# Causal attention ahead of two FFNs: units of 64 queries with both heads stacked on the partitions

## The chip, the cores and the metric

The kernel runs on one core of a Trainium2 chip. The metric is device time in microseconds (us) of one execution, lower is better; the time of before is the median of three runs. The engines are named as the profile names them: PE (TensorE matmuls), PEld (its weight loads), DVE (VectorE), ACT (ScalarE), POOL (GpSimd), SP (SyncE, whose queue issues the DMAs).

## The reference

Batch 2, 12 heads, 448 tokens, 64 elements per head, everything float32 from end to end. Attention is followed by two feed-forward networks.

```python
scores = q @ k.T / sqrt(64)                       # per head
scores = where(key > query, -1e9, scores)         # causal mask
attn = exp(scores - max(scores))
attn = attn / (sum(attn) + 1e-9)
x = (attn @ v)                                    # to [896 tokens, 768]
h = x @ w_in;  x = (h * sigmoid(h)) @ w_out       # 768 -> 2048 -> 768
h = x @ w_in2; solu = h * softmax(h)
x = layernorm(solu) * g @ w_out2                  # 768 -> 1024 -> 768
```

## The kernel before, in words

The kernel has three stages one after another: attention (to about 76 us), the first FFN, the second FFN. The FFNs multiply float32 numbers as sums of three products of rounded parts (`wh`, `wl` for a weight, `h`, `l` for an activation), and their weights arrive packed and have to be converted on ACT, DVE and POOL. The change touches the attention stage and how much of the weight conversion is done in it.

Attention runs over 12 **pairs** of heads (2 batches, 6 pairs each; `p` in the code). A pair's q and k lie with head 0 on partitions 0 to 63 and head 1 on 64 to 127. The work of a pair is cut into seven **units**. In the kernel before these are, for each of the two heads, a unit of 128 queries by 128, by 256 and by 384 keys, and one last unit with the remaining 64 queries of both heads by 448 keys, stacked on the partitions. The steps for a pair, each named by letters in a table:

- `So`, `Sa`, `Sb`, `Sc`: scores on PE (`scores`, L174; the last unit `scores_last`, L184). A matmul uses the 64 rows of its head, which is half of PE's array. The last unit is done in two passes that add into the same tile, and between the passes stands a relay through SP (`f`, L193), so that the two row halves don't write one bank at a time.
- `m`: mask and maximum of a unit, DVE (`maxes`, L204). It reads the scores from PSUM and writes scaled scores to `e` in SBUF.
- `e`: exponential with its row sum, ACT (`exps`, L210).
- `r`: one reciprocal of all the row sums of a pair, DVE (`recip`, L216 and L217).
- `n`: division of a unit by its sum, on POOL (L224), ACT (L222) or DVE (L226), as the letter G, A or V at the step's end says.
- `T`: 16 transposes on PE into one PSUM slot (`transp`, L238), twice per pair. `x`: their eviction to `aT`, on DVE (L253) or ACT (L255).
- `P`: the products with v on PE (`pv`, L264). `h` and `l`: their rounded part (ACT L273, DVE L271) and the rest (DVE L278), which are the input of the first FFN.

Beside these the table holds the loads (`q` L148, `v` L154, `w` L285, all issued by SP in order), steps of the weight conversion for the first FFN (`ca` on ACT, L291; `sh`, `sl`, `rh` on DVE, L308, L296 and L303; `sp` on ACT, L354; `wl` on POOL, L358) and, near the end of the stage, the first blocks of the FFN's first product (`g`, L427 to L429). A chunk of weights is 384 columns on 128 partitions.

The order of all these steps is the string `ORDER` (L60). The engines work off the instructions in the order in which the steps stand there, each engine its own share, and semaphores hold a step back until what it reads is there and what it overwrites is free. Scores, transposes and products with v share four PSUM slots of two banks each (the number after the slash); there are four buffers `e`, four `aT`, four for raw weights.

```python
        for step in ORDER.split():
            step, _, n = step.partition("/")
            e = {"A": nc.scalar, "V": nc.vector, "G": nc.gpsimd}.get(step[-1])
            ...
            emit[name](int(step[len(name):]), int(n) if n else None, u, e)
        fed[0] = EARLY + 1
        pend.append(EARLY)
```

Of the kernel before, what the change touches and what calls it, by code (L numbers as in the profile page):

```python
# [51 lines left out]
UNITS = [(0, 2), (1, 2), (0, 0), (1, 0), (0, 1), (1, 1), (0, 3)]  # L52

# [7 lines left out]
So0/1 Sa0/2 m0.00 m0.10 e0.00 Sb0/0 m0.02 m0.12 e0.02 f0 v5 Sc0 e0.12 v3 e0.10 m0.03 q4 v6 m0.01 Sa1/3 e0.03 m0.11  # L61
e0.01 Sb1/1 m1.10 e0.11 Sb2/2 m1.00 f1 m1.12 v0 Sc1 e1.00 f2 r0 w0 e1.10 m1.02 Sa2/0 n0.10G e1.12 m1.03 n0.12G e1.02
Sc2 m1.11 n0.03G m1.01 e1.03 m2.10 Sa3/3 m2.00 e1.11 m2.12 n0.00G n0.11G e1.01 m2.03 Sb3/1 e2.00 n0.02G m2.02 f3 Sc3
e2.10 m2.11 e2.03 n0.01G r1 Sb4/0 m3.02 e2.11 n1.11G f4 m2.01 q5 e2.12 n1.03G m3.10 v1 T0.0/2 m3.12 e2.02 v7 m3.00
n1.02G m3.11 w1 e2.01 T0.1/3 m3.03 v2 x0.0A Sc4 n1.12G m3.01 v9 r2 x0.1A n1.01G Sa4/1 x0.2V ca0 e3.03 n2.01G x0.3V
T1.1/2 q8 n1.00G e3.10 m4.00 w2 P0/3 m4.10 n2.03G e3.01 m4.01 w3 m4.11 e3.00 m4.03 n2.00G q6 e3.02 n1.10G m4.02
e3.12 n2.11G T1.0/0 m4.12 h0A n2.02G x1.3V Sa5/1 e3.11 n2.12G l0 x1.1A x1.0A x1.2V T2.1/3 n2.10G e4.02 r3 T2.0/0
m5.00 n3.10G e4.11 sh0 P1/2 n3.00G x2.1A x2.3V x2.0A n3.11G m5.12 n3.02G e4.12 x2.2V P2/0 e4.03 m5.10 n3.12G m5.02
h1A sl0 n3.01G e4.10 l1 e4.00 Sb5/3 e4.01 h2V n3.03G T3.0/1 e5.12 f5 q7 r4 T3.1/2 sh1 n4.12G ca3 l2 Sc5 e5.00 x3.2V
x3.0A n4.02G Sa6/0 x3.3V q9 x3.1A n4.11G e5.10 m5.11 Sb6/1 ca1 m6.00 n4.01G m6.12 P3/2 f6 e5.02 v4 n4.03G m5.03  # L70
e5.11 m5.01 e5.03 n4.10G m6.10 m6.02 n4.00G e5.01 T4.1/3 rh0 h3A T4.0/0 sh2 r5 x4.3A Sc6 l3 n5.01G x4.2A sl1 x4.0A
n5.00G Sa7/2 q10 m6.01 x4.1A m6.03 n5.10G e6.12 P4/3 n5.11G m7.00 m6.11 e6.00 n5.12G m7.12 e6.02 m7.02 n5.02G e6.01
m7.10 Sb7/0 h4V e6.10 n5.03G T5.0/1 e7.02 f7 v10 l4 Sc7 e6.11 x5.0V e7.12 T5.1/2 x5.1V e6.03 Sb8/3 rh1 Sa8/1 x5.3A
f8 w4 r6 m7.01 x5.2A n6.02G Sc8 m7.03 e7.00 e7.10 m7.11 n6.01G P5/2 m8.01 e7.01 n6.12G m8.10 sp1 m8.03 e7.11 n6.11G
m8.12 e7.03 m8.02 n6.10G Sa9/0 n6.00G m8.11 h5A n6.03G m8.00 sp0 l5 T6.0/3 e8.01 r7 Sb9/1 e8.12 x6.1V T6.1/2 n7.11G
f9 x6.0V v11 e8.10 Sc9 n7.01G w5 x6.3A m9.02 n7.02G v8 x6.2A P6/3 m9.10 q11 e8.11 m9.11 n7.03G m9.01 n7.00A e8.00
m9.00 n7.12V n7.10G e8.02 m9.03 T7.1/2 wl1 e8.03 m9.12 T7.0/1 x7.2A r8 Sa10/0 x7.3A x7.0V n8.00G n8.10G h6A Sb10/2
n8.01G e9.12 x7.1V m10.00 f10 n8.12G P7/1 l6 e9.10 e9.03 m10.12 n8.11G m10.10 e9.02 n8.02V n8.03G m10.02 e9.00
# [11 lines left out]
def fused(ctx, tc, qk, vv, w1, w2, w3, w4, gl, out):  # L90
# [13 lines left out]
    gain = const.tile([128, KF2], F32, name="gain")  # L104

# [16 lines left out]
    with tc.manual_schedule():  # L122
# [4 lines left out]
        mask3 = att.tile([128, S], F32, name="mask3", bufs=1)  # L127
# [48 lines left out]
        def scores_last(p, n, first):  # L176
            k, q = raws[p]
            if first:
                sb[p] = slot(n)
            dst = scs[p, 0, 3] = sb[p][:, :, 256:256 + S // 2]  # L180
            made = []
            for j in range(2):
                r, z = slice(64 * j, 64 * j + 64), j if first else 1 - j
                made.append(nc.tensor.matmul(dst[:, z], q[QC][r], k[r, S // 2 * z:S // 2 * (z + 1)],  # L184
                                             start=first, stop=not first))
            if first:
                passes[p] = made
            else:
                for m in made:
                    behind(m, relays[p])  # L190

        def relay(p):
            relays[p] = nc.sync.nop(nofuse=True)  # L193
            for m in passes[p]:
                behind(relays[p], m)
# [981 lines left out]
```

## Time and profile before

| | |
|---|---|
| median of 3 runs | 401.11 us (400.26 to 401.73) |
| the profiled execution | 401.01 us |
| its span in the profile | 399.2 us, TensorE clock 1.00 |
| PE, DVE, ACT, POOL busy | 98%, 74%, 70%, 46% of the span |
| DMA | 50.04 MB, mean 125 GB/s |

The profile is one execution. An engine counts as busy from the start of an instruction to its end, and for PE that can hold waits, since matmuls are pipelined. Shares over the whole span average three stages with different limits, so the rows below are taken from windows of the attention stage, and from one window of the FFN for comparison.

### The profile page before, as it was taken

What the parts mean: (1) busy time and instruction counts of PE and PEld (TensorE: products, weight loads), DVE (VectorE), ACT (ScalarE), POOL (GpSimd) and SP (SyncE); (2) the same over time, 40 slices, a digit from 0 to 9 for tenths busy, and PEclk for the clock granted to TensorE, in tenths of its full rate; (3) what the DMA queues carried; (4) which work ended last, traced back from release to release, by engine and by line L of the source; (5) the groups of instructions that cost most, each with busy time, mean ns of one, the idle gap of its engine ahead of it and who ended that gap; (6) DMA issues with size and microseconds to landing.
All of it is one profiled execution on the core that took longest, in us unless ns stands there. A gap on an engine that the chain in (4) does not pass through costs nothing.

```text
span 399.2 us, 7580 instructions
## 1 busy us (share of the span) xinstructions
PE 392.2 (98%) x2622; PEld 363.1 (91%) x2622; DVE 295.9 (74%) x693; ACT 281.1 (70%) x653; POOL 183.9 (46%) x219
## 2 busy tenths in 40 slices
PE   7999999999999999999999999999999999999996
PEld 5777678899999999999999999999988888999996
DVE  4999999677675765768566667776899997666943
ACT  5999999655665473766577777785757875898630
POOL 2998783223554372556665445554001000496450
PEclk9999999999999999999999999999999999999999
DMA  7775322134434333437344567777023320011121
GB/s 246 248 276 173 121 91 65 56 92 151 150 98 125 112 113 112 120 120 201 115 150 129 164 178 233 244 252 217 18 81 98 101 79 0 2 61 39 42 79 61
DMA packets 19766, 50.04 MB, mean 125 GB/s; under 512 B 2320, under 2 KB 4496, under 8 KB 19728
## 3 DMA queue, kind: packets, MB, share of 16 engines
q1 hardware_dynamic: 19728, 49.56, 39.4%
q8 instruction: 21, 0.34, 0.4%
q14 instruction: 17, 0.14, 0.1%
HBM read 46.80 MB, written 2.75 MB: 124 GB/s over the span
## 4 chain that ended last, share of the span: by engine, by line
PE 89%; DVE 8%; ACT 2%; issue 1%; DVEq 0%; ACTq 0%; SPq 0%
PE h L427 8%; PE h L429 8%; PE h L428 8%; PE x L264 5%; PE ps L942 5%; PE h L598 4%; PE h L597 4%; PE h L599 4%; PE ps L944 4%; PE ps L943 4%; PE h L865 3%; PE h L867 3%; PE h L866 3%; PE x L174 3%; PE x L238 3%; DVE e L204 3%
## 5 line engine op out<-in xcount | busy, mean ns | idle before, releaser
L291 ACT ACTIVATE wr<-wr 128x384 f32<-128x384 f32 x96 | 56.9, 592 | 9.4 <-DMA wr<-w_in 9.4
L428 PE MATMUL h<-l,wh 128*128 128x448 f32 x174 | 61.3, 352 | 0.0
L427 PE MATMUL h<-h,wh 128*128 128x448 f32 x174 | 61.3, 352 | 0.0
L429 PE MATMUL h<-h,wl 128*128 128x448 f32 x174 | 61.3, 352 | 0.0
L224 POOL TENSOR_TENSOR e<-e,st 128x128 f32<-128x128 f32 (+3 forms) x70 | 44.0, 666 | 20.1 <-DVE st L217 15.1
L321 DVE SCALAR_TENSOR_TENSOR pw<-wr,pw 128x384 uint32<-128x384 uint32 x77 | 43.0, 559 | 12.9 <-ACT pw L317 12.7
L446 POOL TENSOR_TENSOR gl<-sg,gh 128x448 fp32r<-128x448 f32 x29 | 32.8, 1152 | 38.9 <-ACT sg L444 38.9
L210 ACT ACTIVATE e<-e,st 128x128 f32<-128x128 f32 (+3 forms) x84 | 43.8, 536 | 4.2 <-DVE st L204 4.2
L358 DVE TENSOR_TENSOR wl<-pw,wh 128x384 fp32r<-128x384 f32 x29 | 16.2, 557 | 31.7 <-ACT wh L354 31.7
L354 ACT ACTIVATE wh<-pw 128x384 fp32r<-128x384 f32 x29 | 14.3, 494 | 35.2 <-PE h L428 27.4
L204 DVE CUSTOM_DVE_ANT_0 e<-x,mask 128x128 f32<-128x128 f32 (+3 forms) x84 | 32.9, 445 | 5.2 <-PE x L174 5.1
L428 PEld LDWEIGHTS h<-l,wh 128*128 128x128 f32 x174 | 32.9, 189 | 0.1
L427 PEld LDWEIGHTS h<-h,wh 128*128 128x128 f32 x174 | 32.9, 189 | 0.0
L429 PEld LDWEIGHTS h<-h,wl 128*128 128x128 f32 x174 | 32.9, 189 | 0.0
L896 POOL TENSOR_TENSOR s<-s,mhalf 128x1 f32<-128x1 f32 x7 | 4.2, 596 | 62.3 <-DVE s L895 62.3
L865 PE MATMUL h<-w3h,h 128*128 128x512 f32 x84 | 32.0, 381 | 0.6 <-ACT h L893 0.6
L866 PE MATMUL h<-w3l,h 128*128 128x512 f32 x84 | 31.9, 379 | 0.0
L867 PE MATMUL h<-w3h,l 128*128 128x512 f32 x84 | 31.8, 379 | 0.0
L597 PE MATMUL h<-gh,wh 128*128 128x448 f32 x90 | 31.7, 352 | 0.0
L599 PE MATMUL h<-gh,wl 128*128 128x448 f32 x90 | 31.7, 352 | 0.0
L598 PE MATMUL h<-gl,wh 128*128 128x448 f32 x90 | 31.7, 352 | 0.0
L358 POOL TENSOR_TENSOR wl<-wx,wh 128x384 fp32r<-128x384 f32 x21 | 21.2, 1011 | 22.7 <-ACT wh L354 22.7
(299 smaller groups left out, 1115.1 us busy)
## 6 DMA issues: line engine op xcount, KB each, us to landing
wr<-w_in SPq DMA_DIRECT2D x96, 384.0 KB, 3.2
qk<-qk_in SPq DMA_DIRECT2D x11, 480.0 KB, 4.6
v<-vv_in SPq DMA_DIRECT2D x12, 256.0 KB, 5.2
out<-o SPq DMA_DIRECT2D x14, 192.0 KB, 1.9
qk<-qk_in SPq DMA_DIRECT2D x2, 128.0 KB, 2.3
qk<-qk_in SPq DMA_DIRECT2D x1, 224.0 KB, 2.6
gain<-gl_in SPq DMA_DIRECT2D x1, 4.0 KB, 3.8
```

The lines of the kernel that those rows point to most:

```text
L204: nc.vector.tensor_tensor_reduce(o, scs[p, u[0], u[1]], m, -SCALE, 3.0e38, ALU.add, ALU.min, st[p % 4][:, COL[u]:COL[u] + 1])
L210: nc.scalar.activation(ep(p, u), ep(p, u), AF.Exp, bias=st[p % 4][:, n:n + 1], scale=-1.0, accum_out=st[p % 4][:, 8 + n:9 + n])
L224: eng.tensor_tensor(ep(p, u), ep(p, u), r.to_broadcast([128, wide(u[1])]), ALU.mult)
L291: nc.scalar.activation(high, high, AF.Copy, scale=DOWN)
L427: nc.tensor.matmul(ps[:, :S], wh, rh, start=turn == 0 and k % NB == 0, stop=False)
L428: nc.tensor.matmul(ps[:, :S], wh, rl, start=False, stop=False)
L429: nc.tensor.matmul(ps[:, :S], wl, rh, start=False, stop=turn == 1 and k % NB == NB - 1)
L597: nc.tensor.matmul(ps[:, :S], wh, rh, start=f == CF[0], stop=False)
L598: nc.tensor.matmul(ps[:, :S], wh, rl, start=False, stop=False)
L599: nc.tensor.matmul(ps[:, :S], wl, rh, start=False, stop=f == CF[-1])
L865: nc.tensor.matmul(ps[:, n], yh[k][:, at], wh, start=k == 0, stop=False)
L866: nc.tensor.matmul(ps[:, n], yh[k][:, at], wl, start=False, stop=False)
```

## The change

A unit now holds 64 queries of both heads, head 0 on partitions 0 to 63 of the result and head 1 on 64 to 127. A pair has seven units of 64, 128, ... 448 keys. The scores of a unit are two matmuls of 64 rows by 64 columns of the array; in units 1 to 4 (`SWAPPED`) the heads change places, so that head 0 writes partitions 64 to 127. Unswapped units go to the first bank of each slot, swapped ones to the second (`BANKS`). With that the two passes of the last unit, the relay and the second mask are gone, and q and k of a pair are 448 KB instead of 480.

```diff
-UNITS = [(0, 2), (1, 2), (0, 0), (1, 0), (0, 1), (1, 1), (0, 3)]
+UNITS = S // C
+SWAPPED = (1, 2, 3, 4)
+BANKS = ((6, 0), (4, 2), (5,), (3, 1))
+RUNS = ((0, 1, 0), (1, 5, 1), (5, 7, 0))
...
-        def scores(p, c):
-            k, q = raws[p]
-            for j in range(2):
-                r = slice(64 * j, 64 * j + 64)
-                t = sb[p][:, 1 - j] if c == 1 else sa[p][:, j, 384:] if c == 0 else sa[p][:, j]
-                scs[p, j, c] = dst = t[:, :wide(c)]
-                nc.tensor.matmul(dst, q[c][r], k[r, :wide(c)], start=True, stop=True)
...
+        def scores(p, us):
+            a = raws[p]
+            for u in us:
+                n = next(n for n, bank in enumerate(BANKS) if u in bank)
+                t = (sa, sb)[n // 2][p][:, n % 2]
+                o = sum(wide(v) for v in BANKS[n][:BANKS[n].index(u)])
+                scs[p, u] = t = t[:, o:o + wide(u)]
+                for j in range(2):
+                    r, z = slice(64 * j, 64 * j + 64), 64 * (j ^ (u in SWAPPED))
+                    nc.tensor.matmul(t[z:z + 64], a[r, 0, C * u:C * u + C], a[r, 1, :wide(u)], start=True, stop=True)
```

The products with v follow the swap: three runs of units with one assignment of heads each, 16 matmuls per pair instead of 8, over the same columns. Transposes are evicted by block of keys: pieces of 896, 128, 640 and 384 columns instead of 768, 256, 512 and 512.

```diff
             for z in range(NKB):
-                for j in range(2):
-                    nc.tensor.matmul(t[64 * j:64 * j + 64, 128 * z:S], v[:, j, z], aT[p][:, z, j, 128 * z:],
-                                     start=z == 0, stop=z == NKB - 1)
+                for lo, hi, swap in RUNS:
+                    sl = slice(C * max(lo, 2 * z), C * hi)
+                    for h in range(2):
+                        j = h ^ swap
+                        if sl.start < sl.stop:
+                            nc.tensor.matmul(t[64 * j:64 * j + 64, sl], v[:, j, z], aT[p][:, z, h, sl],
+                                             start=z == lo == 0, stop=z == NKB - 1, skip_group_check=True)
```

The first step of the weight conversion, `ca`, may be put on POOL, as a multiplication by a constant tile `down`; and four chunks instead of five are converted ahead of the FFN stage.

```diff
-        def conv_a(n, c):
+        def conv_a(n, c, eng=None):
             r = wraw[n, c]
             high = r[:, :, 1].bitcast(F32)
-            nc.scalar.activation(high, high, AF.Copy, scale=DOWN)
+            if eng is nc.gpsimd:
+                eng.tensor_tensor(high, high, down.to_broadcast([128, CH]), ALU.mult)
+            else:
+                nc.scalar.activation(high, high, AF.Copy, scale=DOWN)
...
-        fed[0] = EARLY + 1
-        pend.append(EARLY)
+        fed[0] = EARLY
```

The table is written anew throughout: another order, another share of the engines (norms, up to the last reciprocal: 64 columns on ACT, 1152 on DVE, the rest on POOL; `ca0` to `ca4` on POOL; `h9` to `h11` on DVE), loads in the order q1 v0 q2 v1 q3. One line of it:

```diff
-e2.10 m2.11 e2.03 n0.01G r1 Sb4/0 m3.02 e2.11 n1.11G f4 m2.01 q5 e2.12 n1.03G m3.10 v1 T0.0/2 m3.12 e2.02 v7 m3.00
+Sb4/3 x1.2V x1.1A n2.5G e3.6 P1/0 m4.2 q8 m4.1 n2.3G e3.5 m4.5 v7 m4.4 ca0G e4.1 r3 e4.4 m4.3 T2.1/2 n3.1G n3.4V h1A
```

On PE, one pair early in the stage; `x` is a PSUM slot, `qk` a pair's q and k, `e` its exponentials, `aT` the transposes, `v` its v. Before:

```order
L184 MATMUL x_258<-qk 128x224 x2
L174 MATMUL x_258<-qk 128x256 x2
L174 MATMUL x_334<-qk 128x384 x2
L174 MATMUL x_334<-qk 128x128 x2
L238 MATMUL x_344<-ident,e_98 128x64 x16
L264 MATMUL x_368<-aT,v_196 64x448 x2
L264 MATMUL x_368<-aT,v_196 64x320 x2
L264 MATMUL x_368<-aT,v_196 64x192 x2
L264 MATMUL x_368<-aT,v_196 64x64 x2
```

and now:

```order
L160 MATMUL x_311<-qk 64x448 x2
L160 MATMUL x_311<-qk 64x320 x2
L160 MATMUL x_311<-qk 64x192 x2
L160 MATMUL x_311<-qk 64x64 x2
L160 MATMUL x_324<-qk 64x384 x2
L160 MATMUL x_324<-qk 64x256 x2
L160 MATMUL x_324<-qk 64x128 x2
L225 MATMUL x_336<-aT,v_146 64x64 x2
L225 MATMUL x_336<-aT,v_146 64x256 x2
L225 MATMUL x_336<-aT,v_146 64x128 x2
L225 MATMUL x_336<-aT,v_146 64x192 x2
```

The result of a scores matmul now has 64 partitions instead of 128 (its first number), seven pairs of matmuls stand together where the passes of L184 were apart, and the products with v come in more and shorter pieces.

The step `ca` early in the table stood on ACT among the exponentials (`wr` is a chunk of raw weights):

```order
L210 ACTIVATE e_97,st_101<-e_97,st_101 128x256
L210 ACTIVATE e_98,st_102<-e_98,st_102 128x384
L291 ACTIVATE wr<-wr 128x384
L210 ACTIVATE e_98,st_102<-e_98,st_102 128x128
L255 ACTIVATE aT<-x_514 128x2x384
L255 ACTIVATE aT<-x_514 128x2x128
```

and stands now on POOL, between the norms of one pair and the next:

```order
L184 TENSOR_TENSOR e_99<-e_99,st_103 128x384
L184 TENSOR_TENSOR e_99<-e_99,st_103 128x256
L253 TENSOR_TENSOR wr<-wr,down 128x384
L184 TENSOR_TENSOR e_100<-e_100,st_104 128x128
L184 TENSOR_TENSOR e_100<-e_100,st_104 128x192
```

Norms that stood behind `ca` in no queue now stand behind it on POOL.

## Rows read from the trace of the kernel before

**Rows 1.** Windows: length, busy PE, PEld, DVE, ACT, POOL, clock, DMA share, GB/s.

```profile
4.50:16.65 12.15, 10.80 (x96) 7.72 (x92) 10.08 (x55) 10.41 (x39) 5.81 (x10) 1.00 0.76 274
16.65:62.15 45.50, 45.32 (x605) 33.25 (x605) 44.80 (x169) 45.37 (x151) 36.91 (x58) 1.00 0.49 167
...
80.00:100.00 20.00, 20.00 (x107) 19.98 (x106) 14.93 (x30) 11.43 (x27) 5.75 (x6) 1.00 0.41 123
```

**Rows 2.** The chain in order of time, one pair: start us, us, what.

```profile
28.78 0.99 PE x L238 x32
29.77 0.43 PE x L184 x4
30.21 1.30 PE x L174 x12
31.51 0.38 PE x L184 x4
31.89 1.88 PE x L264 x16
```

**Rows 3.** Groups by shape on ACT, 3 to 77 us: busy us, mean ns, idle before.

```profile
L210 ACT ACTIVATE e<-e,st 128x384 f32<-128x384 f32 x24 | 14.8, 620 | 0.9 <-DVE st L204 0.9
...
L210 ACT ACTIVATE e<-e,st 128x128 f32<-128x128 f32 x24 | 9.6, 406 | 2.8 <-DVE st L204 2.8
...
L273 ACT ACTIVATE h<-x 128x448 fp32r<-128x448 f32 x8 | 4.3, 542 | 3.8 <-PE x L264 3.8
```

**Rows 4.** Groups by shape on DVE, 3 to 77 us.

```profile
L204 DVE CUSTOM_DVE_ANT_0 e<-x,mask 128x384 f32<-128x384 f32 x24 | 12.8, 547 | 0.6 <-PE x L174 0.6
...
L253 DVE COPY aT<-x 128x512 f32<-128x512 f32 x14 | 9.2, 676 | 0.6 <-PE x L238 0.6
...
L278 DVE TENSOR_TENSOR l<-x,h 128x448 fp32r<-128x448 f32 x12 | 7.4, 615 | 0.4 <-ACT h L273 0.3
...
L204 DVE CUSTOM_DVE_ANT_0 e<-x,mask 128x128 f32<-128x128 f32 x24 | 6.6, 286 | 3.2 <-PE x L174 3.2
```

**Rows 5.** Timeline of ACT around one ca: start us, us, instruction.

```profile
29.24 0.59 ACT L291 ACTIVATE wr<-wr 128x384 f32<-128x384 f32 x1
...
29.71 0.41 ACT L210 ACTIVATE e<-e,st 128x128 f32<-128x128 f32 x1
```

**Rows 6.** Groups by shape on POOL, 3 to 77 us.

```profile
L224 POOL TENSOR_TENSOR e<-e,st 128x384 f32<-128x384 f32 x16 | 13.0, 828 | 2.7 <-DVE st L217 2.3 <-PE x L238 0.4
...
L224 POOL TENSOR_TENSOR e<-e,st 128x128 f32<-128x128 f32 x22 | 9.3, 437 | 14.7 <-DVE st L217 10.8 <-ACT e L210 3.9
L358 POOL TENSOR_TENSOR wl<-wx,wh 128x384 fp32r<-128x384 f32 x4 | 4.0, 1008 | 1.6 <-ACT wh L354 1.6
```

**Rows 7.** Timeline of POOL, seven norms in the middle; in brackets the idle time before.

```profile
42.12 4.37 POOL L224 TENSOR_TENSOR e<-e,st 128x384 f32<-128x384 f32 x7 [2.30 <-DVE st L217]
```

**Rows 8.** Timeline of all engines, the start.

```profile
7.76 0.62 DVE L204 CUSTOM_DVE_ANT_0 e<-x,mask 128x448 f32<-128x448 f32 x1 [1.04 <-PE x L174]
...
10.47 0.21 DVE L217 RECIPROCAL st<-st 128x9 f32<-128x9 f32 x1
```

**Rows 9.** Timeline of all engines, the end of the attention stage.

```profile
68.54 0.21 DVE L217 RECIPROCAL st<-st 128x9 f32<-128x9 f32 x1
...
70.62 1.31 PE L238 MATMUL x<-ident,e 64*128 64x64 f32 x32
...
71.47 2.15 DVE L253 COPY aT<-x 128x512 f32<-128x512 f32 x3 [0.57 <-PE x L238]
...
73.99 1.95 PE L264 MATMUL x<-aT,v 128*64 128x448 f32 x16
...
75.87 0.46 PE L427 MATMUL ps<-h,wh 128*128 128x448 f32 x1
```

**Rows 10.** The chain in order of time, two FFN blocks among the pairs.

```profile
62.22 0.39 PE ps L427
...
65.82 1.25 PE x L238 x32
```

More of the change, by code (lines that the diff above doesn't have):

```diff
@@ L69 @@
[L69 to L78, printed above, removed]
@@ L176, in scores_last @@
[L176 to L181, printed above, removed]
-            for j in range(2):
[L183 to L195, printed above, removed]
+        sa, sb = {}, {}
+        def scores(p, us):
[8 more added lines that the diff above has]
+                    nc.tensor.matmul(t[z:z + 64], a[r, 0, C * u:C * u + C], a[r, 1, :wide(u)], start=True, stop=True)
@@ L216, in recip @@
-            nc.vector.tensor_scalar(more, t[:, 8:17].rearrange("q (a b) -> q a b", b=9), 1e-9, None, ALU.add)
-            nc.vector.reciprocal(t[:, 32:41].rearrange("q (a b) -> q a b", b=3), more)
+            nc.vector.tensor_scalar(t[:, 8:8 + UNITS], t[:, 8:8 + UNITS], 1e-9, None, ALU.add)
+            nc.vector.reciprocal(t[:, 16:16 + UNITS], t[:, 8:8 + UNITS])
         def norm(p, u, eng):
-            r = st[p % 4][:, 32 + COL[u]:33 + COL[u]]
+            r = st[p % 4][:, 16 + u:17 + u]
             if eng is nc.scalar:
@@ L505, in g1drain, with scores_to, first_scores @@
             gemm1(f, half, 0, turn)
-        def scores_a(p, n):
-            sa[p] = slot(n)
-            for c in (2, 0) if p else (2,):
-                scores(p, c)
-        def scores_ahead(p, n):
-            sa[p] = slot(n)
-            scores(p, 0)
+        def scores_to(tiles, p, n, us):
+            if n is not None:
+                tiles[p] = slot(n)
+            scores(p, us)
+        def first_scores(p, n):
+            sb[p] = slot(1)
+            scores_to(sa, p, n, (0, 1))
         emit = {
-            "So": lambda p, n, u, e: scores_ahead(p, n), "Sa": lambda p, n, u, e: scores_a(p, n), "Sb": lambda p, n, u, e: scores_last(p, n, True),
-            "Sc": lambda p, n, u, e: (scores_last(p, n, False), scores(p, 1)), "f": lambda p, n, u, e: relay(p),
+            "Sx": lambda p, n, u, e: first_scores(p, n), "Sy": lambda p, n, u, e: scores(p, (2, 3)),
+            "Sz": lambda p, n, u, e: scores(p, (4, 5, 6)),
+            "Sa": lambda p, n, u, e: scores_to(sa, p, n, (6, 4, 2, 0)), "Sb": lambda p, n, u, e: scores_to(sb, p, n, (5, 3, 1)),
             "q": lambda p, n, u, e: load_pair(p), "v": lambda p, n, u, e: load_v(p),
@@ L1141, in heads_T @@
         return a.transpose(0, 1, 3, 2).reshape(B, NP, 128, S)
-    cut = 128 * (NKB - 1)
     q, k = heads_T(inputs["q"]), heads_T(inputs["k"])
-    last = np.zeros((B, NP, 2, D, 2, C), np.float32)
-    for j in range(2):
-        last[:, :, j, :, j] = q[:, :, D * j:D * j + D, cut:]
     v = np.zeros((B, NP, 2, 128 * NKB, D), np.float32)
```

118 lines of the change are left out of this document (50 added, 68 removed).

## The prediction

> **What bounds the kernel now.** I read the windows first, then the chain, one head pair of it in order of time, and last the price list of each engine. In 16.65 to 62.15, most of the attention stage, four engines are nearly full at once: of 45.50 us PE has 45.32, ACT 45.37, DVE 44.80, and POOL 36.91. From 80 on only PE is full (20.00 of 20.00; DVE 14.93, ACT 11.43) [rows 1]. So work that leaves DVE or ACT is worth something in the attention stage and nothing after it; the change wins or loses before the dense stage begins. The chain of waits runs over PE there, but a busy PE record also holds waiting, so I count PE's work from the chain's pieces for one head pair: 0.99 transposes, 1.30 scores, 0.43 and 0.38 the two passes of the last unit, 1.88 the products with v, together 4.98 us [rows 2]. Twelve pairs are 59.8, less than the stage lasts. ACT and DVE show no such slack: I take them as the pace, with PE close behind.
>
> **The change, part by part.** Columns per pair fall from 1984 (two heads of 128, 256 and 384 keys, one unit of 448) to 1792 (64 to 448 in steps of 64), 2304 less in twelve pairs; there are 7 units either way.
> - Exponentials (ACT): 406 ns at 128 columns, 620 at 384 [rows 3], 0.84 ns per column: 2304 columns are **-1.9 us**.
> - Maxima (DVE): 286 and 547 ns [rows 4], 1.02 ns per column: **-2.4**.
> - Evictions of the transposes: up to its last exponential ACT has 20 instead of 22 and 1024 columns less, at the exponentials' 0.84 ns 0.9, with the two instructions **-1.0**. DVE has one more and 256 columns more; half of the 676 ns that one of 512 takes [rows 4], **+0.3**.
> - Norms: ACT had four before its last exponential (128, 384, 128, 384 columns) and has one of 64. A 384-column operation of 0.59 us is followed after 0.47 [rows 5], so 0.12 of each record overlaps the next. By the exponentials' 0.41 and 0.62, less 0.12 each, 1.6 go and 0.3 come: **-1.3**. DVE's norms have 1152 columns instead of 1792; at most the maxima's 1.02 ns, 0.65, which also read a mask; I take **-0.4**.
> - Output halves: three h move from DVE to ACT before its last exponential, 542 ns less 0.12 [rows 3]: **+1.3**. DVE loses two casts (three instead of one before) and gains one subtraction l. A subtraction of that size is 615 ns, a cast reads one operand less but is as long in columns [rows 4]: **-1.2** and **+0.5**.
> - Weight conversion: four ca leave ACT, 0.47 each [rows 5]: **-1.9**. One chunk fewer is converted ahead, three operations of 384 columns leave DVE, each like a maximum of that size, 0.5 with overlap [rows 4]: **-1.5**. They return in the dense stage, covered by DVE's 5 idle us in 20 [rows 1]; without that cover they cost 1.5.
>
> ACT up to the last exponential: -1.9 - 1.0 - 1.3 + 1.3 - 1.9 = **-4.8**. DVE up to the last reciprocal: -2.4 + 0.3 - 0.4 - 1.2 + 0.5 - 1.5 = **-4.7**.
>
> *POOL goes the other way.* A norm is 437 ns at 128 columns and 828 at 384 [rows 6]: 242 ns and 1.53 per column. Four more norms with 64 more columns are 1.0 us, five ca, the same kind of multiplication, 4.1: **+5.1**. In the middle window its work becomes 42.0 us, where 45.5 - 4.7 = 40.8 would remain [rows 1].
>
> *PE.* The scores become quarters of 64 rows by 64 columns. Today two row halves run side by side, 768 columns per head in 1.30 us [rows 2], 1.69 ns per column. With all four quarters at once 1792 columns are 896 column times, 1.51 us, where scores now take 2.11: **-0.6 per pair**. The trace before shows no four at once, so the other bound is two at a time: 1792 x 1.69 = 3.03, **+0.9 per pair**. I take the first, as the nearer rows are both halves of what is asked: row halves run side by side in the scores, column halves in the products with v (1024 columns per head in 1.88 us [rows 2]), and the table alternates unswapped and swapped units. The products with v go from 8 to 16 instructions with the same columns. Their 1.88 is 0.15 above 1024 x 1.69; I allow 0.05 for the added entries, with 0 and another 0.15 as bounds. PE then has 4.4 to 4.6 per pair and hides beside the others. The relay through SP goes; what is late next is the slot, whose maxima must all be done before the next pair's scores enter.
>
> *The sum for the stage.* If ACT and DVE kept their packing it would be -4.7. But POOL's 42.0 don't fit into 40.8: 1.2 of the gain is lost unless POOL falls behind, which four e buffers permit (bound 0). POOL has also waited for a reciprocal, up to 2.30 us [rows 7]; one such wait more makes 3.5 (the other bound). I take back 1.5: **-3.2**.
>
> *The start.* The last unit of pair 0 gets its maximum at 7.76, the first reciprocal is at 10.47 [rows 8]. Now a maximum waits for all matmuls of its slot, which at the start delays the first ones; in return the two-pass unit and its relay are gone. Pair 2's q and k follow 160 KB later in the queue, at 274 GB/s [rows 1] 0.6 us, and are wanted only after pair 1's maxima. I put the start at 0, bounds -0.5 and +0.7.
>
> *The tail.* From the last reciprocal at 68.54 to the last products with v at 73.99 are 5.45 us [rows 9]. Now POOL norms 128, 320 and 384 columns in a row, 0.44 + 0.73 + 0.83 = 2.0 [rows 6]; the transposes take 1.31 as before; the evictions, of which DVE alone had 2.15 [rows 9], are split over ACT and DVE, 1.2; hand-overs 0.2: together 4.7, **-0.7**.
>
> All of it: -3.2 - 0.7 + 0.1 (entries of the last products) = **-3.8**. The profiled execution took 401.01 us, 0.1 below the median of 401.11: 397.2 against itself, **397.3** against the median.
>
> **The rivals.** *A, the forecast:* quarters overlap, ACT and DVE set the pace. Its own range is 395.3 (nothing taken back, the start 0.5 better) to 399.2 (3.5 taken back).
>
> *B, slower: the quarters don't overlap and PE becomes the pace.* Both heads of a unit are two row halves that write one bank. The kernel before never lets that happen: its heads write different banks, and the two passes of the last unit wait for each other. At two at a time a pair costs 4.98 + 0.9 + 0.05 = 5.95 us, twelve 71.4. Two FFN blocks take 3.6 (62.22 to 65.82 [rows 10]), the three ahead of the last products 5.4. From the first scores at 3.6 that ends at 80.4 with no wait at all, and at 83.5 with 3 us of waiting at the start, against 75.87 [rows 9]: +5 to +9, **408**. It decides from about 2.9 us of scores per pair, where PE's twelve pairs and FFN blocks again last as long as the stage before. For it: the shared bank. Against it: halves run side by side wherever the trace has them, and the two heads write different partitions.
>
> The Trainium skill, "TensorEngine Tiling (Array Packing)", section "Gotcha 1: PSUM Pressure", states that "different row tiles cannot access same PSUM bank simultaneously". By that rule a unit's two heads could not run together, and the sum would be B's. No run here shows two row halves in one bank; the trace agrees only so far that the kernel before, which has them in two banks, overlaps them.
>
> *C, no change: POOL takes over.* Before pair 11 POOL has 70 norms of 18304 columns, 44.9 us, five ca 4.1, and two wl at 1.0 [rows 6]: 51 us from the first reciprocal at 10.47 [rows 8], that is to 61.5 without any wait. Before, it was idle for 8.6 us of the middle window alone [rows 1]. With 7 us of such idle left, pair 11's norms begin at 68.5, as before: 400.4; with 5 to 9, 399 to 402.5. For it: ca stands in POOL's queue ahead of norms for which transposes wait. Against it: POOL has work of several pairs in its queue once it lags, so it should wait less.
>
> **How the numbers follow.** Chances: A 0.60, C 0.22, B 0.18. A difference below 0.5%, 2.0 us, can hardly be told from none here: faster is below 399.1, slower above 403.1. A lies in the first, C nearly whole between, B in the last: 0.60, 0.22, 0.18. The time is A's, 397.3. The range reaches from 394.6 (A's lower end, less 0.7 for terms taken at the middle of their bounds, DVE's norms and the tail) to 403.0 (C's upper end and most of what the start could add); it leaves out B.
>
> **What would show it.** Right: the pieces of scores for one pair sum to about 1.5 us in the chain; the last exponential is near 63 and the last reciprocal near 65 instead of 68.54; POOL is full in the middle window; the first reciprocal at 10 to 11; the dense stage has the same length, only begins some 4 us sooner. Wrong: scores of about 3 us per pair and DVE waiting for them (B); the last reciprocal near 68 with transposes waiting for POOL (C); POOL's 384 columns far above 828 ns; or a dense stage that lengthens for want of the fifth converted chunk.

## The result, and the profile after

The changed kernel takes 404.34 us in the median of five runs (402.87 to 404.66), against 401.11 before: ratio 1.0078, interval 1.006 to 1.0096, so **slower by 0.8%** where 397.3 was forecast. The profiled execution took 402.87 us, the shortest of the five; its span is 400.6 us against 399.2.

The span divides at five marks that both traces have: the first, fourth and tenth reciprocal (pairs 0, 3 and 9) and the first FFN block on PE.

| us | before | after | difference |
|---|---|---|---|
| to the first reciprocal | 10.47 | 11.02 | +0.55 |
| first to fourth | 13.32 | 14.74 | +1.42 |
| fourth to tenth | 33.03 | 31.43 | -1.60 |
| tenth to the first FFN block | 5.32 | 6.09 | +0.77 |
| from there to the end | 337.09 | 337.37 | +0.28 |

So the gain that was forecast exists, in the middle, and nearly twice as much is lost at the two ends. The two traces differ by 1.4 us, the medians by 3.2, as the profiled execution is the fastest of the five. Three of the edits below (`e7`, `e8`, `e16`) leave the start of the table as the change has it, and their traces show slower starts: first reciprocal at 11.51, 12.62 and 11.61, from there to the fourth 15.03, 15.02 and 15.43 us. In all four traces the fourth reciprocal is 2.0 to 3.9 us later than before (23.79).

Windows of the trace after (length, busy PE, PEld, DVE, ACT, POOL, granted clock, DMA share, GB/s):

```profile
4.00:11.00 7.00, 6.15 (x81) 3.83 (x76) 3.54 (x19) 3.98 (x15) 0.00 (x0) 1.00 0.97 345
11.00:15.20 4.20, 0.51 (x12) 0.22 (x4) 4.17 (x22) 4.20 (x19) 3.82 (x7) 1.00 1.03 410
...
17.00:20.00 3.00, 3.00 (x36) 1.93 (x30) 1.77 (x8) 2.39 (x9) 2.36 (x4) 0.57 0.72 271
...
25.00:63.00 38.00, 36.33 (x697) 29.56 (x695) 36.56 (x145) 36.75 (x128) 33.31 (x53) 1.00 0.30 96
63.00:77.30 14.30, 14.22 (x199) 12.16 (x194) 12.85 (x30) 9.06 (x25) 8.27 (x11) 1.00 0.28 85
```

The same for the trace before, two of these stretches and its own last one:

```profile
11.00:15.20 4.20, 4.11 (x40) 3.21 (x36) 4.17 (x23) 4.20 (x17) 4.20 (x8) 1.00 0.70 264
...
17.00:20.00 3.00, 3.00 (x48) 2.35 (x46) 2.96 (x13) 3.00 (x10) 3.00 (x6) 1.00 0.90 311
...
62.15:75.87 13.72, 13.72 (x143) 10.27 (x139) 12.77 (x33) 9.81 (x28) 5.23 (x8) 1.00 0.20 60
```

From 11.0 to 15.2 PE was busy 0.51 us where it had been busy 4.11. Behind that its granted clock falls from 1.00 to 0.57 in the mean of 17 to 20 us, that is, to 1.2 GHz for most of it, and DVE and ACT, full up to then, wait. The timeline after shows what PE waited for, and in its last line that DVE in turn waited for the scores of pair 3:

```profile
7.55 0.36 DVE L166 CUSTOM_DVE_ANT_0 e<-x,mask 128x192 f32<-128x192 f32 x1 [1.74 <-PE x L160]
...
11.02 0.20 DVE L177 RECIPROCAL st<-st 128x7 f32<-128x7 f32 x1
...
11.38 4.04 POOL L184 TENSOR_TENSOR e<-e,st 128x128 f32<-128x128 f32 x7 [7.61 <-DVE st L166]
...
15.22 1.22 PE L198 MATMUL x<-ident,e 64*128 64x64 f32 x30 [1.97 <-POOL e L184]
...
16.37 3.26 PE L160 MATMUL x<-qk 64*64 64x448 f32 x28
...
18.43 0.49 DVE L166 CUSTOM_DVE_ANT_0 e<-x,mask 128x320 f32<-128x320 f32 x1 [1.23 <-PE x L160]
```

Scores of three pairs are done at 11.2. Next in PE's order stand the transposes of pair 0, which wait for seven norms that all stand on POOL, 4.04 us of work. Scores of pair 3, behind them, then take 3.26 us at the low clock. Before, these transposes came no earlier, at 15.84; but there the scores, two at a time and with more columns, filled PE up to them:

```profile
15.84 1.52 PE L238 MATMUL x<-ident,e 64*128 64x64 f32 x32 [0.43 <-DVE st L204]
```

In the steady part of the changed kernel (chain in order of time) the same step, the first line, takes half of that:

```profile
43.21 1.67 PE x L160 x18
44.88 1.91 PE x L225 x32
46.79 1.31 PE x L198 x32
```

1.67 us is near the 1.51 forecast for four quarters and far from 3.03; before it was 2.11 [rows 2].

### The profile page after: what moved, and what is told of

Read it like the earlier page. It is cut to its first block, busy times and chain, and to the rows that moved or that the text cites. A ratio compares the mean times of both kernels' runs of the same rounds, so it can differ in the third digit from the quotient of the medians.

```text
span 400.6 us, 8157 instructions
## 1 busy us (share of the span) xinstructions
PE 388.9 (97%) x2910; PEld 364.3 (91%) x2910; DVE 295.0 (74%) x689; ACT 278.2 (69%) x648; POOL 189.5 (47%) x235
## 4 chain that ended last, share of the span: by engine, by line
PE 82%; DVE 10%; ACT 4%; POOL 2%; DMA 1%; issue 1%; SPq 0%; DVEq 0%; ACTq 0%
PE h L393 8%; PE h L392 8%; PE h L391 8%; PE ps L900 5%; PE h L555 4%; PE h L557 4%; PE h L556 4%; PE ps L902 4%; PE ps L901 4%; PE h L823 3%; PE x L160 3%; PE h L825 3%; PE h L824 3%; ACT e L171 3%; PE x L225 2%; DVE w3l L322 2%
## 5 line engine op out<-in xcount | busy, mean ns | idle before, releaser
L255 ACT ACTIVATE wr<-wr 128x384 f32<-128x384 f32 x91 | 53.9, 593 | 10.3 <-DMA wr<-w_in 10.0
L184 POOL TENSOR_TENSOR e<-e,st 128x128 f32<-128x128 f32 (+6 forms) x74 | 44.5, 635 | 17.2 <-DVE st L166 9.4
L171 ACT ACTIVATE e<-e,st 128x320 f32<-128x320 f32 (+6 forms) x84 | 41.8, 501 | 8.0 <-DVE st L166 7.7
L166 DVE CUSTOM_DVE_ANT_0 e<-x,mask 128x128 f32<-128x128 f32 (+6 forms) x84 | 31.1, 415 | 8.2 <-PE x L160 7.8
L391 PEld LDWEIGHTS h<-h,wh 128*128 128x128 f32 x174 | 32.9, 189 | 0.1
L393 PEld LDWEIGHTS h<-h,wl 128*128 128x128 f32 x174 | 32.9, 189 | 0.0
L392 PEld LDWEIGHTS h<-l,wh 128*128 128x128 f32 x174 | 32.9, 189 | 0.0
```

Of the source, the lines that this page charges most:

```text
L171: nc.scalar.activation(ep(p, u), ep(p, u), AF.Exp, bias=st[p % 4][:, u:u + 1], scale=-1.0, accum_out=st[p % 4][:, 8 + u:9 + u])
L184: eng.tensor_tensor(ep(p, u), ep(p, u), r.to_broadcast([128, wide(u)]), ALU.mult)
L255: nc.scalar.activation(high, high, AF.Copy, scale=DOWN)
L391: nc.tensor.matmul(ps[:, :S], wh, rh, start=turn == 0 and k % NB == 0, stop=False)
L392: nc.tensor.matmul(ps[:, :S], wh, rl, start=False, stop=False)
L393: nc.tensor.matmul(ps[:, :S], wl, rh, start=False, stop=turn == 1 and k % NB == NB - 1)
```

## The experiments

All are edits of the changed kernel; the kernel before had medians of 400.96 to 401.19 beside them. "Stretches" are those of the table above. An edit is called not told apart from another when the intervals of their ratios overlap. Diffs of the table show only the part of its lines that changes.

**Quarters.** SWAPPED empty, one run of products with v:

```diff
-SWAPPED = (1, 2, 3, 4)
-RUNS = ((0, 1, 0), (1, 5, 1), (5, 7, 0))
+SWAPPED = ()
+RUNS = ((0, 7, 0),)
```

> No unit is swapped: head 0 is always row half 0 and column half 0, head 1 the other two, so only two of the four quarters are used, and the products with v go back to 8 matmuls per pair. Theory (the quarters overlap, two heads in one bank do no harm): scores of a pair take 3.0 us instead of 1.7, PE becomes the pace, time up by 5 to 9 us, to 409 to 413. Rival 1 (quarters bring nothing here, as the stage is limited elsewhere): scores 3.0 us, time within 2 us of 404. Rival 2 (two row halves in one bank are kept apart): scores of a pair about 6 us, time above 430.

413.78 us, ratio 1.0321 (1.0306 to 1.0336). One pair's scores in its chain in order of time:

```profile
48.58 3.17 PE x L160 x28
```

and its window of the middle:

```profile
25.00:63.00 38.00, 37.45 (x458) 23.37 (x456) 29.25 (x118) 30.35 (x101) 26.04 (x45) 1.00 0.29 95
```

3.17 us for a pair: two at a time, side by side though both heads write one bank; DVE falls from 36.56 to 29.25 of 38. Theory held, at a little over its price. The four quarters do work, and are worth 9.4 us here (413.78 against 404.34).

The Trainium skill, "TensorEngine Tiling (Array Packing)", "Gotcha 1: PSUM Pressure", says that row tiles can't access one PSUM bank at the same time. Both traces differ, for two heads that write different partitions of the bank, and the measurement decides: 3.17 us is the price of two at a time in one bank (two separate banks gave 1792 x 1.69 = 3.03), and 1.67 that of four.

**Who paces the middle.** `ca0` to `ca4` without their G, that is, on ACT:

```diff
-n3.1G n3.4V ... ca0G
+n3.1G n3.4V ... ca0
```

> The five first conversion steps are put back on ACT, in the same places of the table; POOL loses 4.4 us of work, ACT gains 2.4. Theory (the middle is paced by ACT and DVE, POOL follows): the reciprocals of pairs 3 to 10 lie 0.5 to 2 us further apart in sum than 37.4 us, time 404 to 406. Rival (POOL is the pace of the middle): they lie 2 to 4 us closer, time 400 to 402.

404.88 us (ratio 1.009, 1.0072 to 1.0109). Fourth to eleventh reciprocal 38.33 instead of 37.37, and in its window POOL has 28.43 where it had 33.31, ACT 37.40 where it had 36.75:

```profile
25.00:63.00 38.00, 35.27 (x672) 28.44 (x666) 35.37 (x143) 37.40 (x128) 28.43 (x49) 1.00 0.31 100
```

POOL has five steps of 894 ns less to do, 4.5 us, and nothing comes earlier; ACT has more, and the marks come later. The theory held in its numbers. As one edit moved both, it shows that POOL isn't the pace, and not that ACT alone is. The trace of the change says the same of POOL, which waits for a reciprocal between two pairs (timeline):

```profile
42.22 4.04 POOL L184 TENSOR_TENSOR e<-e,st 128x320 f32<-128x320 f32 x7 [0.43 <-DVE st L177]
```

PE's three pieces above, 4.89 us for a pair, follow one another without a gap from 43.14 to 52.80; of these 9.66 us ACT has 9.37 and DVE 9.09. There PE is as near to being the pace as they are, which the prediction had not expected (4.4 to 4.6 a pair, hidden).

**The clock and the idle stretch.** Matmuls of zeros ahead of the first transposes (`k14/3`: fourteen into slot 3):

```diff
-e2.2 n0.0G v5 T0.1/3 r1
+e2.2 n0.0G v5 k14/3 T0.1/3 r1
...
+            for _ in range(count):
+                nc.tensor.matmul(t[:, :S], xl[0][:, :128], xl[0][:, :S], start=True, stop=True)
```

> Fourteen matmuls of zeros into a free slot stand on PE before the first transposes, where PE stood idle from 11.2 to 15.2 us while POOL divided pair 0; nothing else is changed. Theory (the idle stretch costs the clock, and the half clock that follows costs about half of its own length): the granted clock stays 1.00 from 15 to 20 us, the scores of pair 3 take 1.7 instead of 3.2 us, the third reciprocal comes 1 to 2 us earlier than 20.62, and the time falls by 1 to 3 us to 401 to 403. Rival (the loss is the starving alone, the clock is only a symptom): clock 1.00, but the later reciprocals where they were within 0.3 us and 404 as before.

403.88 us, ratio 1.0066 (1.0045 to 1.0088), not told apart from the change. In its profile the zeros had to wait for a slot and came too late; windows of it show the clock at 0.88 and then 0.50:

```profile
11.00:15.20 4.20, 2.29 (x24) 1.83 (x15) 3.73 (x22) 4.20 (x18) 2.92 (x5) 0.88 1.02 398
15.20:17.00 1.80, 1.80 (x7) 1.59 (x6) 1.59 (x11) 1.80 (x7) 1.65 (x5) 0.50 1.03 404
```

But its six runs split: 402.42 and 402.76 with a mean granted clock of 1.000, 403.25 with 0.998, and 404.51, 405.01 and 405.17 with 0.996. One program, **2.3 us** between the two groups. That is more than the clock alone can cost: 0.004 of 402 us is 1.6 us of PE's time (an estimate), and the start differs from run to run as well. In the seven later programs with runs of both kinds (from 0.998 up, and below) the runs with the lower clock are longer by 0.5 to 1.7 us in the mean. So a fall of the clock goes with a longer time, but its price is not isolated, and the theory, whose zeros came too late, is not tested by this run. All five runs of the change had 0.992 to 0.996, the runs of the kernel before 0.998 to 1.000.

**Scores of pair 3 first**, slots of the first pairs renamed:

```diff
-v5 T0.1/3 r1 e2.3 m2.0 n1.2G n1.0V T0.0/2 e2.4 m2.1
+v5 Sa3/0 Sb3/1 r1 e2.3 m2.0 n1.2G n1.0V T0.1/2 e2.4 m2.1 T0.0/3
```

> The scores of pair 3 are issued ahead of pair 0's transposes (the slots of the first pairs renamed for it), so PE has real work in the idle stretch. Theory: no half clock, and 1.7 us of PE work leave the stretch after 15.2, so the third reciprocal comes 2 to 2.7 us earlier than 20.62 and the time is 400 to 402. Rival (POOL sets the pace from the first norm on, PE's idle time is harmless): the first and second reciprocal as before, the fourth within 0.5 us of 25.76, time 404.

402.48 us, ratio 1.004 (1.0026 to 1.0054), clocks 0.998 to 1.000: 1.9 us less than the change, with intervals apart. PE idles about as long in sum behind 11 us (4.1 us instead of 3.7), but with work in between (timeline):

```profile
14.59 1.74 PE L160 MATMUL x<-qk 64*64 64x448 f32 x28 [1.97 <-issue]
17.26 1.21 PE L198 MATMUL x<-ident,e 64*128 64x64 f32 x32 [0.93 <-DVE st L166]
```

First to fourth reciprocal 13.84 instead of 14.74, 0.5 above before. But the first one came at 12.61 here, as PE's matmuls ran slowly for longer at the start. Groups by shape on PE from 7.3 to 9.6 us, where a scores matmul of 448 columns takes 951 ns:

```profile
L160 PE MATMUL x<-qk 64*64 64x448 f32 x6 | 2.5, 951 | 0.0
```

and in the trace of the change from 6.5 to 9.4, where it takes 536:

```profile
L160 PE MATMUL x<-qk 64*64 64x448 f32 x8 | 1.7, 536 | 0.0
```

**Zeros at the start**, alone and with the edit above:

```diff
-WARM = 5
+WARM = 6
-m0.1 Sy0 m0.0
+m0.1 k2 Sy0 m0.0
```

> One more matmul of zeros ahead of the first scores (6 instead of 5) and two between the first two units and the rest of pair 0, where PE waited for a load from 4.0 to 4.6 us; nothing else. In the four traces of this table the first scores matmul at full rate (536 instead of 951 ns at 448 columns) came between 5.0 and 9.6 us and the first reciprocal followed it, between 11.0 and 12.6. Theory (PE is too idle at the start to be given its clock in time): full rate by 5.8 us, first reciprocal 10.4 to 11.0, the runs lie closer together, and the time falls by 0.5 to 1.5 us to 403 to 404. Rival (the loads set the start): first reciprocal not before 11.0, time as before, 404.3.

404.06 us (1.0058 to 1.0086). Full rate at 5.3 us, but first reciprocal 11.36: no gain, against the theory. The added zeros put the first scores 0.37 us later (3.92 instead of 3.55), and the clock still fell behind the idle stretch (0.995 and 0.996 in all runs).

> The scores of pair 3 ahead of the first transposes (as in the earlier run of this edit) together with the matmuls of zeros at the start. The earlier run lost 2.1 us against the kernel before up to the first reciprocal (12.61 against 10.47) and ended 2.1 us later. Theory (start and idle stretch are two separate losses that add): first reciprocal 10.4 to 11.2, granted clock 1.00 throughout, time 400 to 401.2, equal to the kernel before. Rival (the time stays at 402.5 as the loads set the start): first reciprocal 12 or later.

403.1 us (1.0033 to 1.0058). First reciprocal 11.20, but now the clock fell at 18 us, as windows of the profile show:

```profile
18.00:19.00 1.00, 0.77 (x8) 0.58 (x10) 1.00 (x5) 1.00 (x6) 1.00 (x3) 0.64 1.02 390
19.00:21.00 2.00, 2.00 (x20) 1.66 (x18) 1.97 (x14) 1.52 (x8) 1.28 (x3) 0.50 1.04 390
```

The losses don't simply add: the theory's 401.2 at most was missed, as what the start gave, the clock took three pairs later, in some of the runs (three had a mean clock of 1.000 and took 402.53 to 403.10, two of 0.995 and 0.996 took 403.21 and 403.53). From the first to the fourth reciprocal this trace needs 14.89 us, more than the change, where the traces with pair 3's scores first and no fall of the clock (`e2`, `e13`, `e15`) need 13.82 to 14.28. So in that stretch the new order gains only where the clock also holds.

**Fillers into unused columns** (`z7.2`: seven into the slot of pair 2's scores), and early maxima with them:

```diff
-v5 Sa3/0 Sb3/1 r1
+v5 z7.2 Sa3/0 Sb3/1 r1
...
+                nc.tensor.matmul(sb[p][:, 0, 384:512], ident, ident, start=True, stop=True)
```

> The edit of the run before (scores of pair 3 first, zeros at the start) plus sixteen multiplications of the unit matrix by itself into unused columns of a scores bank, at the three places between 11 and 18 us where PE still stood idle for 0.9 to 1.5 us and after which the clock fell to 0.50 at 18.2 us in that run. Theory (idle PE costs its clock): granted clock 1.00 in every window up to 25 us, 13.3 to 14.0 us from the first to the fourth reciprocal instead of 14.9, the first FFN block 1 us earlier than 63.63, time 401.5 to 402.5. Rival (the clock falls for another reason, such as power of the DMA burst): clock below 0.9 somewhere in 15 to 22 us, time 403.

406.58 us. The fillers waited for DVE's maxima of the slot that they shared and held up the scores behind them (timeline):

```profile
14.84 1.80 PE L476 MATMUL x<-ident 128*128 128x128 f32 x14 [2.87 <-DVE st L166]
16.57 1.74 PE L160 MATMUL x<-qk 64*64 64x448 f32 x28
```

This says nothing for either side: the clock stayed at 1.00 in this profile in spite of 2.87 us of idling, other runs had 0.996.

> As the last, and the maxima of units 2 and 3 of pair 0 stand ahead of the scores of its units 4 to 6 in the table, so that they need not wait for unit 6, with three more matmuls of zeros in the wait that this puts on PE. Theory (the first reciprocal is late because a maximum waits for every matmul issued to its slot before it): first reciprocal 10.4 to 10.8 instead of 11.2, and the same 0.4 to 0.8 us off the time. Rival (DVE's seven maxima are bounded by the last load): first reciprocal 11.0 or later, time as the last.

406.41 us, confounded by the same fillers; the first reciprocal came at 11.74, not at 10.4 to 10.8.

**POOL's chain of pair 0 shortened.**

```diff
-r0 q5 m1.1 e1.2 n0.1G
+r0 q5 m1.1 n0.6V e1.2 n0.1G
-m1.6 v4 e1.3 m1.5 n0.2G Sb2/1 e1.6 m1.0 n0.5G
+m1.6 n0.5V v4 e1.3 m1.5 n0.2G Sb2/1 e1.6 m1.0
```

> Two of pair 0's seven norms (units 5 and 6) go from POOL to DVE, right behind the first reciprocal, so that POOL's chain ahead of the first transposes is 2.4 instead of 4.0 us; scores and slots as in the change. Theory (PE stands idle because the transposes wait for POOL's norms of pair 0): the transposes begin 2.5 to 3 us after the first reciprocal instead of 4.2, 13.3 to 14.2 us from the first to the fourth reciprocal instead of 14.7, granted clock mean 0.998 to 1.0 in most runs, time 402 to 403. Rival (the slots of the scores hold PE, not POOL): transposes 4 us after the reciprocal or later, time 404.

403.36 us (1.0046 to 1.0074), 1.0 us below the change, but not told apart from it. The transposes begin 2.6 us after the reciprocal (11.22) instead of 4.2, so they had waited for POOL. But nothing came of it: the scores of pair 3 start at 16.36 as they did at 16.37, the clock falls all the same (0.990 to 0.996), and the stretch to the fourth reciprocal takes 14.64 instead of 14.74 (timeline):

```profile
13.79 1.51 PE L198 MATMUL x<-ident,e 64*128 64x64 f32 x32 [2.60 <-DVE st L166]
16.36 3.16 PE L160 MATMUL x<-qk 64*64 64x448 f32 x28 [1.06 <-issue]
```

What PE waits for in those 1.06 us the same trace shows: pair 3's scores enter the slot of pair 2, whose last maximum (64 columns) stands on DVE behind the second reciprocal and ends at 16.26. In the change it ended at 15.52, and the transposes held the scores for another 0.85 us. Here the two norms on DVE put it 0.7 us later and give back what POOL's shorter chain had gained. So both sides of the question were half right: the transposes wait for POOL, the next scores for the transposes or for their slot, whichever is later.

**Early maxima** with pair 3's scores first, and with the norms on DVE:

```diff
-Sy0 m0.0 v2 e0.1 e0.0 Sz0 m0.2 m0.3 e0.2 m0.4
+Sy0 m0.0 m0.2 v2 e0.1 e0.0 m0.3 e0.2 Sz0 m0.4
```

> Scores of pair 3 first, as in the earlier run of that edit (402.48), and the maxima of units 2 and 3 of pair 0 ahead of the scores of units 4 to 6, with no zeros multiplied anywhere. Theory (the first reciprocal is late because these maxima wait for unit 6): from the first scores at 3.55 the reciprocal comes 0.4 to 0.8 us sooner than in that run at the same moment of full rate, time 401.7 to 402.2. Rival (the wait that PE gets in exchange costs as much, and the clock comes later): time 402.4 or more.

402.26 us (1.0024 to 1.0051), not told apart from 402.48.

> The two norms on DVE and the early maxima together, on the changed kernel. Theory (POOL's chain of pair 0 and the late first reciprocal are separate): 0.4 to 0.8 us below the first of these runs, 401.3 to 402.5. Rival (DVE, which gets both, is late for pair 1 instead): not below it.

402.44 us (1.0025 to 1.0061). It is 0.9 below the run of the norms alone, with overlapping intervals; first reciprocal 11.09. In the traces of the change and of all its edits the first reciprocal lies between 11.02 and 12.62, never at the 10.47 of before.

**The end.** `h9V`, `h10V` and `x11.3V` on ACT:

```diff
-e11.3 h9V T10.0/1
+e11.3 h9A T10.0/1
```

> Two rounded halves (pairs 9 and 10) and one eviction of pair 11 go from DVE to ACT, which was busy 9.06 of the last 14 us. Theory (the end is paced by DVE): the last reciprocal comes about 0.5 us sooner after the one before it (6.38 us), the last products with v end 7.0 instead of 7.85 us after it, time 402.5 to 403.5. Rival (the end is paced by POOL's norms and the transposes behind them): both within 0.3 us of before, time 404.

404.22 us; the last products with v end 7.98 us after the last reciprocal, 7.85 in the change: nothing gained, against the theory. POOL's norms of the last pairs left out:

```diff
-l7 e10.3 n9.3G x8.3V x8.0A Sa11/0 n9.2G x8.2V n9.1G
+l7 e10.3 x8.3V x8.0A Sa11/0 x8.2V
```

> POOL's norms of pairs 9, 10 and 11 are left out (14 of its 74), so those rows of the attention are not divided by their sums; everything else stands. Theory (DVE and POOL slow each other when both read SBUF twice): on DVE the operations of L267, 911 ns in the mean, fall to about 560, and the norms of 256 and 448 columns, 1.71 us together, to about 1.0; the last reciprocal comes 1 to 1.5 us earlier after the tenth. Rival (those operations are slow for another reason, their own operands): L267 stays at 850 to 950 ns. The time is shorter in either case, as transposes no longer wait for POOL: 400 to 402.

One run, 403.55 us; as its first reciprocal came only at 12.62, the time says little. Groups by shape on DVE, 57 to 77 us, in the change:

```profile
L267 DVE SCALAR_TENSOR_TENSOR wx<-wr,wx 128x384 uint32<-128x384 uint32 x3 | 2.9, 965 | 0.0
...
L186 DVE TENSOR_SCALAR e<-e,st 128x448 f32<-128x448 f32 x1 | 1.0, 1012 | 0.0
```

and without those norms:

```profile
L267 DVE SCALAR_TENSOR_TENSOR wx<-wr,wx 128x384 uint32<-128x384 uint32 x3 | 1.6, 538 | 0.0
...
L186 DVE TENSOR_SCALAR e<-e,st 128x448 f32<-128x448 f32 x1 | 0.5, 450 | 0.0
```

That these operations are slower beside POOL's norms is shown: 965 and 538 ns, 1012 and 450. Yet only 0.46 us of the stretch behind the tenth reciprocal comes back (5.63), and 0.25 from the first FFN block to the end (337.12).

Two steps of the weight conversion moved:

```diff
-m11.2 n9.0A sl1 sp0 n9.6G m10.0 e11.0 rh1 Sb11/1 h8A wl0 m11.4 e10.0 T9.1/2
+m11.2 n9.0A sp0 n9.6G m10.0 e11.0 Sb11/1 h8A wl0 m11.4 sl1 e10.0 T9.1/2 rh1
```

> As the last, and two steps of the weight conversion on DVE (0.60 and 1.07 us in the chain at 60 to 62 us) stand behind the last maximum of pair 11 instead of ahead of it. Theory (from the tenth reciprocal to the first FFN block DVE is the pace, slowed by POOL beside it, and from that block on PE is): 5.4 to 5.8 us instead of 6.1 for that stretch, 0.3 to 0.6 us off the time; from the block to the end 337.4 us as in all runs. Rival (POOL's norms of pair 9 hold the transposes there): 6.0 us or more, no change.

406.98 us, as this run still holds the fillers of the two above; 6.44 us instead of 6.09, as the FFN block now waited 0.74 us for a subtraction queued behind the two steps. Moved behind that as well (`l8 T9.0/0 sl1 rh1`):

> Scores of pair 3 first and the early maxima (402.26 in the run before), and two steps of the weight conversion on DVE stand behind the last maximum of pair 11 and behind the subtraction that frees the slot of the first FFN block; in the earlier run of such an edit that subtraction came late in their place. Theory (from the tenth reciprocal to the first FFN block DVE is the pace): 5.4 to 5.8 us for that stretch instead of 6.09, time 401.6 to 402.0. Rival (POOL's norms of pair 9 are the pace there): 6.0 us or more, time 402.3.

402.27 us (1.0021 to 1.0045), where the same kernel without this edit had 402.26.

> The same two steps moved, on the changed kernel and nothing else. Theory: 5.4 to 5.8 us from the tenth reciprocal to the first FFN block, 337.4 us from there to the end, time 403.6 to 404.1 where the change had 404.3. Rival: 6.0 us or more, time as the change's.

403.53 us (1.0042 to 1.0066), not told apart from the change. In both traces the stretch takes 5.63 us, as the theory said, and from the FFN block to the end it is 337.80 instead of 337.37: **given back**. The two steps now stand ahead of pair 10's reciprocal on DVE, for which POOL waits before its norms (timeline of POOL in the last run):

```profile
65.05 2.59 POOL L184 TENSOR_TENSOR e<-e,st 128x128 f32<-128x128 f32 x4 [1.47 <-DVE st L177]
```

and PE's transposes of that pair, behind the FFN block, wait 0.37 us for these norms, as they don't in the change.

None of the sixteen beats the kernel before; the best (402.26 and 402.27) are 0.3 to 0.4% above it.

## Why the prediction was wrong, point by point

- **Shown right:** four quarters overlap (1.67 us; without swaps 3.17, and 9.4 us more than the change), so rival B's premise is gone. The middle gained 1.60 us in six pairs, where 3.2 over eleven would be 1.75. The dense stage has its old length: from the first FFN block behind the last products with v to the end it takes 323.4 us before and 323.3 after, so the chunk converted later costs nothing there.
- **Right by luck:** the take-back of 1.5. Its reason was that POOL's 42.0 us don't fit into 40.8. But POOL has 33.31 of 38 us in the window from 25 to 63 and waits for reciprocals there, and 4.5 us less on POOL brought no gain; so C's premise fails for the middle too. No engine is full in that window any more: DVE 36.56, ACT 36.75, PE 36.33 of 38.
- **The step that failed first: "I put the start at 0, bounds -0.5 and +0.7".** The first reciprocal came 0.55 later, within the bounds, but the sum of the start ended there. The loss was behind it: 1.42 us more to the fourth in the fastest execution, 1.7 to 2.1 in the three other traces with this start. I had read PE's 0.6 us less per pair as work that "hides beside the others". With its scores faster, PE ran out of them at 11.2. What stood next in its order were transposes behind POOL's whole pair, 4.04 us, and then scores whose slot DVE frees only at 15.52. Both were in the prediction without a price: seven norms of 64 to 448 columns add up to 4.4 by its own rows [rows 6], and "what is late next is the slot" was said of the stage. I had weighed POOL against the stage, never against the first pair. Then the clock fell. Issuing the scores of pair 3 first gives 1.9 of the 3.2 us back; shortening POOL's chain alone gives nothing that can be told apart. How much of the 1.42 is the fall of the clock and how much the late scores isn't separated.
- **The second: the tail, "-0.7".** From the last reciprocal to the start of the last products with v it is 5.58 us (69.52 to 75.10) where it was 5.45 and 4.7 was forecast. It was summed as a chain from the last reciprocal. But from the first FFN block PE is full to the end of the stage, 13.72 of 13.72 us before, and after without a gap from 63.28 to 77.30. The tail's sum has no FFN block in it, and so missed that these blocks make PE the bound there, as long as nothing comes later: three operations of DVE moved to ACT gained nothing. In the traces of the change and of its first fourteen edits the remainder from that block is 337.1 to 337.5 us; most of these edits leave what stands there as it was. The block's start counts, and that came 0.77 later in its stretch; 0.46 of it goes when POOL's late norms are left out, or when two of DVE's steps are moved, which costs as much behind it. The remainder itself is 0.28 longer, and the records of PE account for it: three times the products with v take 0.5 us more in sum, two rounds of transposes 0.2 less.
- **Prices:** the largest error of size is DVE's. Its records up to the last reciprocal fell from 61.33 to 59.42 us, -1.9 where -4.7 was summed; ACT's up to its last exponential from 62.57 to 58.88, -3.7 where it was -4.8. The last reciprocal came at 69.52 instead of near 65, the last exponential at 68.2 instead of 63. ca on POOL is 894 ns (taken 0.83), the norm of 384 columns 848 (828); DVE's conversion steps up to 965 in the mean of a kind (taken 0.5 each). Exponentials fell from 43.8 to 41.8 us, as forecast (-1.9), the maxima from 32.9 to 31.1, less than forecast (-2.4):

```profile
L171 ACT ACTIVATE e<-e,st 128x320 f32<-128x320 f32 (+6 forms) x84 | 41.8, 501 | 8.0 <-DVE st L166 7.7
...
L166 DVE CUSTOM_DVE_ANT_0 e<-x,mask 128x128 f32<-128x128 f32 (+6 forms) x84 | 31.1, 415 | 8.2 <-PE x L160 7.8
```

  The idle time in the last column is where part of the work that was saved went: DVE waits 7.8 us for scores, in the page of before 5.1.
- **Open:** why the first reciprocal is late by half a microsecond and more even with early full rate. With early maxima and no fillers it was 11.09 to 11.44, no earlier than the 11.02 of the change. The time of full rate moves it (11.02 with full rate from about 5.9 us, 12.62 from about 9.7, with the same table up to there), but the kernel before had 10.47 with full rate only from about 6.6. In the change a maximum of pair 0 waits 1.74 us for PE up to 7.55 (first line of the timeline after). Units of one load that fall on the same quarters (2 and 3 both swapped, 5 and 6 both unswapped) do run one after the other in the trace of the change (units 2 and 3 start at 4.63 and 5.32, 5 and 6 at 5.89 and 6.59); that this makes the reciprocal late isn't tested. Why the clock falls after some idle stretches and not after others of about the same length is open as well.

## What to carry to other kernels

An engine that is made faster in a pipeline filled from a cold start needs something to do there: look at what stands next in its own queue at the first hand-over, pair 0, and at the longest chain that feeds it, not at shares over the stage. When a stage ends in a stretch where one engine is full, sum the change to the beginning of that stretch, and behind it count that engine's own work. And before you take the releaser that a trace names for the cause, shorten its work and look whether the next mark moves: here the transposes came 1.4 us sooner, and the scores behind them no sooner, since the work that was moved held up the slot that they enter.

## What the runs showed of the hardware

- Two row halves write one PSUM bank side by side, on different partitions: 1792 columns of float32 scores for each of two heads in 3.17 us. All four quarters together do them in 1.67 us.
- After 4.2 us with 0.51 us of matmuls PE's granted clock fell to 1.2 GHz; after 2.87 us without any it stayed at 1.00 in one profile. At the first scores matmuls ran slower (951 against 536 ns) while the row of the granted clock said 1.00. The change to full rate came anywhere from 5.0 to about 10 us in different traces.
- A scalar_tensor_tensor of 384 columns on DVE, which reads two SBUF operands, took 965 ns beside POOL's two-operand norms and 538 without them; a division of 448 columns by its sums took 1012 and 450. The Trainium skill, "GPSIMD Engine Reference", "1. Specifications", says that POOL shares its SBUF interfaces with VectorE, with contention for two SBUF inputs or a two-port mode. The trace of the first operation agrees; in which mode the second ran no run here shows.
